# Earlier weight loads and a moved preparation of sink values in an attention + MoE + MLP kernel

## The chip, the cores and the metric

One Trainium2 chip, one core of it. The metric is the device time of one execution of the kernel, in microseconds (us), lower is better. Engines are called as the profile calls them: PE (TensorE, matrix products), DVE (VectorE), ACT (ScalarE), POOL (GpSimd), SP (SyncE, which here only issues DMAs).

## The reference

Three steps, all in float32; what one gives is the input of the next.

```python
# 1. attention: batch 2, 8 heads, 768 positions, head size 64
keep = (pos[None, :] < n_sink) | ((rel >= 0) & (rel < window))    # n_sink 4, window 128
a = softmax(where(keep, q @ k.T / 8, -1e9)); x = a @ v            # x: 1536 tokens x 512
# 2. mixture of 8 experts (512 -> 1024 -> 512), each token to its best one
active = x @ w_skip > 0; e = argmax(x @ w_gate); g = softmax(x @ w_gate)[e]
x[active] += g * (relu(x @ w1[e]) @ w2[e])
# 3. rational MLP, 512 -> 2048 -> 512
h = x @ w_in; out = (P3(h) / (1 + |b0||h| + |b1|h*h + 1e-6)) @ w_out
```

n_sink and window come as data. The kernel has a fast way for values that fit (n_sink up to 4, window up to 128) and a general one; a flag, `tripi`, chooses, and every engine loads it into a register (`values_load`) before the first scores.

## The kernel before, in words

The schedule is written by hand: instructions stand on each engine in the order in which the Python code emits them, and strings of steps such as `ORDER` set how steps of neighbouring units interleave.

**Attention** works on 8 pairs of heads. `attend(p)` runs from p = -2 to 10 and emits one round of `ORDER`, in which a step marked @-1 belongs to the pair before and @1 to the pair after. For a pair, PE transposes q and k (`tr`, tiles tq and tk), DVE and ACT copy them out of PSUM (`ev_q`, `ev_k`), POOL copies the four sink columns of K beside every later key tile (`k_sinks`), PE makes scores (`scores`, tile sc), DVE masks them and takes the row minimum (`mask_min`), ACT exponentiates (`expo`), PE transposes the result (`tr_p`, tile pt), and `pv` multiplies with v. The sinks' part of the product, `pv_sink`, needs the sinks' columns (copied by POOL into ps, transposed by `sink_t`) and the sinks' values v, spread over block rows: `sink_values` prepares these once for all pairs, as a PE product with a selection matrix (vsps <- sel), an ACT copy and a DVE subtraction into vsr, and four POOL multiplications by a mask of rows into vs. All of that stands ahead of the comparisons that make `tripi`. The rotated PSUM tiles with the tag tp (4 buffers) serve tq, tk, pt, vsps and the products alike.

At the start of `attend(p)`, SP issues the loads of q and k of pair p + 2 and whatever `after(u)` asks for (u = 2p and 2p + 1). The results go to DRAM (xd <- xs), per pair and half, and DVE or POOL adds up the router's logits lg.

**Routing** follows: DVE finds the best expert and the rank of each token, PE sums ranks (rkp, cntp), `slot_sel` compares ranks with a row of numbers for 12 token tiles (r; `SS` shares the tiles out: DVE up to SS[1] in groups of SS[0], POOL up to SS[2], ACT the rest), PE turns that into the token numbers of each expert's block (idps), and POOL gathers the first three blocks from xd (xblk).

**Experts**: 9 blocks of 128 tokens (8 experts and one for tokens beyond the first 128 of an expert). Each takes 8 chunks of weights of 512 KB (wch). Chunks 0, 1, ... go in order into rooms: s0 to s5 (`NSA` = 6, a pool that lives from the start), r0 to r9 (`NRING`), then s6 to s25 (`NSB` = 20, a pool `wsb` that lies where the attention's tiles were). After these 36, rooms r0 to r9, s24 and s25 are used again and again as their chunks have been used. 16 chunks are loaded in the attention (`after`, two per u from 7 to 14), 7 right behind it (`load_more(NPRE1 + NPRE2)`), 13 behind the gathers (`load_more(..., True)`: a memset by POOL, which stands behind the gathers in POOL's queue, holds the first of these loads, and the others follow it on SP).

Rooms s0 to s23 then take the MLP's weights (wc). These come as raw float64 words (raw, 512 KB each, 3 buffers), are turned by DVE into float32 (ta) and split by ACT and DVE into a high and a low part, one or a few per step from block 2 on. The MLP ends the kernel.

Of the kernel before, what the change touches and what calls it, by code (L numbers as in the profile page):

```python
# [9 lines left out]
F32 = mybir.dt.float32  # L10
F32R = mybir.dt.float32r
# [4 lines left out]
ALU = mybir.AluOpType  # L16
# [8 lines left out]
T = S // 128  # L25
# [11 lines left out]
EMPTY = 4096.0  # L37
ZROW = (E + NOV) * 128
NRING = 10
NSA = 6  # L40
NSB = 20
NCM = 24
ORDER = """
s0 Q1 e14@-1 c0@-1 s1 e15@-1 m00 O1@-2 K1 o0@-2 c1@-1 m10 p02@-1 O0@-2 p00@-1 P02@-1 p01@-1 m01 P00@-1 p12@-1 m11
# [1 line left out]
v4@-1 e12 v5@-1 e03 k0@1 w0@-1 s4 x0@-1 x1@-1 K0@1 s5 m04 e13 q0@1 x2@-1 g0@1 m05 e04 p10 Q0@1 q1@1 o1@-1 P10 m14 e05  # L46
m15 k1@1
"""
NPRE1 = 4
NPRE2 = 3  # L50
LAG = 3
PRE = 2
ML = 1
# [10 lines left out]
M0-3 M1-3 t0-4 A00 A10 P00 M2-3 A20 D00 D10 C30 C00 A5-1 t1-3 C40 t3-3 A30 C10 P1-1 A40 C20 D20 D30 D40  # L64
t2-3 C50 E00 g01
"""
SS = (4, 8, 10)
CRAW = 3
BLOCK = """
L2-1 G00 b03 L3-1 a00 o00 T00 U00 G10 V00 L40 x01 a10 T10 U10 F00 L50 F10 X01 V10 T20 U20 F20 F30 V20 L60 T30 U30  # L70
# [13 lines left out]
def emit(nc, tc, ctx, q, k, v, n_sink, window, w_skip, w_gate, w1, w2, w_in, w_out, pa, pb, out):  # L84
# [61 lines left out]
    def tokens_out(pr, half, ps, sb_pool, sb_tag, sb_bufs, eng=sp):  # L146

        b, c = divmod(pr, KC)
        n = T // 2
        xs = (sb_pool if eng is sp else xbp).tile(  # L150
            [128, n, 128], F32, tag=sb_tag if eng is sp else "xblk", name="xs", bufs=sb_bufs if eng is sp else 3
        )
        ls = sb_pool.tile([128, n, 2, E + 1], F32, tag=sb_tag + "l", name="ls", bufs=sb_bufs)
        r = ri[:, 2 * pr:2 * pr + 2, n * half:n * half + n].rearrange("p h (t o) -> p t h o", o=1)
        dve.tensor_tensor(
            xs.rearrange("p t (h d) -> p t h d", h=2), ps[:, :, 0:128].rearrange("p t (h d) -> p t h d", h=2),
            r.to_broadcast([128, n, 2, D]), op=ALU.mult,
        )
        dve.tensor_tensor(
            ls, ps[:, :, 128:NX].rearrange("p t (h e) -> p t h e", h=2), r.to_broadcast([128, n, 2, E + 1]), op=ALU.mult  # L160
        )
        l = lg4[:, b, half]
        eng_l = dve if pr == NPAIR - 1 and half else pool
        for h in range(2):
            eng_l.tensor_tensor(l, l, ls[:, :, h, :], op=ALU.add)
        r0 = (b * T + n * half) * 128
        eng.dma_start(xd[r0:r0 + n * 128, c * 128:(c + 1) * 128].rearrange("(t p) c -> p t c", p=128), xs)
# [24 lines left out]
    at.tile([128, T, KS], F32, tag="K", name="room", bufs=2)  # L192


    vs8 = at.tile([8, NPAIR, 128], F32, tag="P", name="vs8", bufs=4)
    vsr = at.tile([96, NPAIR, 128], F32R, tag="P", name="vsr", bufs=4)
    vs = at.tile([96, T - 2, NPAIR, 128], F32R, name="vs")

    rows = at.tile([96, T - 2], F32, name="rows")
    sel8 = at.tile([8, 3, 2, T - 2, 4], F32, name="sel8")  # L200
# [32 lines left out]
    def sink_values():  # L233
# [8 lines left out]
        for n in range(2):  # L242
# [5 lines left out]
            r = vsr[:, pr].rearrange("p a c -> p (a c)")  # L248
            act.copy(r, ps)
            dve.tensor_tensor(r[32:64], ps[32:64], r[32:64].bitcast(F32), op=ALU.subtract)  # L250
        for t in range(T - 2):
            pool.tensor_scalar(vs[:, t], vsr.bitcast(F32), rows[:, t:t + 1], None, op0=ALU.mult)

    Qt, Kt = {}, {}
    tp_cur = {}
# [124 lines left out]
    def pv_sink(pr):  # L380
        for t in range(T - 2):
            c, q0 = divmod(t, 2)
            q0 = 256 - 128 * c + 128 * q0
            pe.matmul(xps[pr][c][:, q0:q0 + 128], vs[:, t, pr, :], PS[pr], start=False, stop=t % 2 == 1)

    NU = 2 * NPAIR
    xT = {}
# [38 lines left out]
    def attend(p):  # L426
# [10 lines left out]
            load_v(p + 2)  # L437
        if p == 0:
            dve.tensor_scalar(upper, iota_r, pid, None, op0=ALU.is_gt)

# [31 lines left out]
    pool.memset(m1[:, 128:132], BIG)  # L474
    operands(1)
    k_sinks(0)
    sink_values()

    fast = ct([128, 1], F32, "fast")
    tripi = ct([128, 1], I32, "tripi")  # L480
# [65 lines left out]
    def after(u):  # L546
        if u == 0:
            router_loads()
        if u == 4:
            pab_loads()  # L550
        if NU - 9 <= u < NU:
            for _ in range(2):
                if len(wchunks) < NSA + NRING:
                    e, c = wq.pop(0)
                    load_chunk(e, c, w1[e], w2[e])

    for p in range(-2, NPAIR + 3):
        attend(p)
# [7 lines left out]
    def load_more(n, behind=False):  # L566

        for _ in range(n):
            e, c = wq.pop(0)
            load_chunk(e, c, w1[e], w2[e], behind=behind)  # L570
            behind = False
# [18 lines left out]
                tokens_out(pr, half, tokens_mm(pr, half, xTg[:, pr], gps, "g1"), gp, "gkeep", 1)  # L590
    gps_st.close()
    gp_st.close()
    load_more(NPRE1 + NPRE2)

    psr, psr_st = open_pool("psr", space=PSUM)
    psxt, psxt_st = open_pool("psxt", bufs=4, space=PSUM)
# [97 lines left out]

    for e in range(3):
        get_block(e, idx0[:, e:e + 1])
    load_more(NSB - NPRE1 - NPRE2, True)
    cnt9 = tk.tile([128, E1], F32, name="cnt9")
    dve.tensor_copy(cnt9, cntp)
    cnt, n_pass = cnt9[:, 0:E], cnt9[:, E:E1]  # L700
# [699 lines left out]
```

## Time and profile before

| what | value |
|---|---|
| median of 3 runs (lowest to highest) | 566.01 us (565.42 to 567.33) |
| the profiled execution | 566.55 us, of which its trace spans 564.8 us |
| mean granted clock of PE, as a share of full speed | 0.967 |
| busy share of the span: PE, DVE, ACT, POOL | 92%, 70%, 56%, 28% |
| DMA moved over the span | 83.52 MB, 148 GB/s on average |

Times inside the trace count from the span's start. A busy engine is one that has an instruction running; idle time ahead of an instruction is listed with what ended it. The attention lies at about 5 to 119 us, the routing at 119 to 134, the expert blocks at 134 to 280, the MLP from 268 to the end. PE is granted one of two clocks, 1.2 and 2.4 GHz, which a stretch's PEclk shows as 0.50 and 1.00.

### The profile page before, as it was taken

What the parts mean: (1) busy time and instruction counts of PE and PEld (TensorE: products, weight loads), DVE (VectorE), ACT (ScalarE), POOL (GpSimd) and SP (SyncE); (2) the same over time, 40 slices, a digit from 0 to 9 for tenths busy, and PEclk for the clock granted to TensorE, in tenths of its full rate; (3) what the DMA queues carried; (4) which work ended last, traced back from release to release, by engine and by line L of the source; (5) the groups of instructions that cost most, each with busy time, mean ns of one, the idle gap of its engine ahead of it and who ended that gap; (6) DMA issues with size and microseconds to landing.
All of it is one profiled execution on the core that took longest, in us unless ns stands there. A gap on an engine that the chain in (4) does not pass through costs nothing.

```text
span 564.8 us, 8147 instructions
## 1 busy us (share of the span) xinstructions
PE 517.7 (92%) x2800; PEld 404.2 (72%) x2800; DVE 392.8 (70%) x826; ACT 317.0 (56%) x648; POOL 160.2 (28%) x230
## 2 busy tenths in 40 slices
PE   4599999944999999988999979889999999999995
PEld 2488777734777777766687858678888888888883
DVE  3557767746013676655479999988987888987772
ACT  2568888810112333322557776757767677767671
POOL 2902111225610201011014334525333412522223
PEclk9989999975999999999999979989999999999998
DMA  8637899339999779999213112111000100100001
GB/s 168 133 72 147 238 270 319 126 115 397 314 272 362 269 274 385 415 411 389 102 58 111 57 37 93 39 37 57 19 20 19 38 1 2 74 1 0 1 0 74
DMA packets 73146, 83.52 MB, mean 148 GB/s; under 512 B 43977, under 2 KB 50121, under 8 KB 73098
## 3 DMA queue, kind: packets, MB, share of 16 engines
q1 hardware_dynamic: 67050, 69.41, 38.4%
q0 software_dynamic: 3664, 10.77, 5.8%
q10 hardware_dynamic: 2384, 2.76, 1.4%
q8 instruction: 24, 0.39, 0.3%
q14 instruction: 24, 0.20, 0.1%
HBM read 71.62 MB, written 11.29 MB: 147 GB/s over the span
## 4 chain that ended last, share of the span: by engine, by line
PE 32%; DVE 15%; issue 2%; ACT 2%; POOL 0%; POOLq 0%; DVEq 0%; ACTq 0%
PE hT L1106 16%; PE acc L1158 15%; DVE w L1146 2%; DVE w L1144 2%; DVE w L1131 1%; DVE p L1142 1%; DVE p L1140 1%; DVE p L1148 1%; DVE ta L847 1%; DVE ta L846 1%; DVE wc L833 1%; DVE ta L845 1%; DVE zx L956 1%; DVE zl L964 0%; POOL out L683 0%
## 5 line engine op out<-in xcount | busy, mean ns | idle before, releaser
L1106 PE MATMUL hT<-zh,wc 128*128 128x512 f32 x384 | 131.7, 404 | 5.2 <-DVE p L1142 3.3
L1134 POOL TENSOR_TENSOR gl<-p,gh 128x512 fp32r<-128x512 f32 x46 | 62.2, 1351 | 161.6 <-ACT gh L1126 72.0
L1158 PE MATMUL acc<-wc,gh 128*128 128x512 f32 x368 | 94.3, 397 | 1.2 <-ACT gh L1126 1.2
L1106 PEld LDWEIGHTS hT<-zh,wc 128*128 128x128 f32 x384 | 73.6, 192 | 22.5 <-DVE p L1142 3.5
L1158 PEld LDWEIGHTS acc<-wc,gh 128*128 128x128 f32 x368 | 69.8, 190 | 18.3 <-ACT gh L1126 1.6
L1106 PE MATMUL hT<-zl,wc 128*128 128x512 f32 x192 | 76.7, 399 | 3.2 <-DVE zl L964 3.2
L880 PEld LDWEIGHTS hps<-xbT,wch 128*128 128x128 f32 x576 | 68.4, 198 | 4.9 <-issue 3.6
L880 PE MATMUL hps<-xbT,wch 128*128 128x128 f32 x576 | 68.8, 282 | 0.7 <-ACT xbT L870 0.7
L891 PE MATMUL yps<-wch,hT 128*128 128x512 f32 x144 | 64.3, 594 | 2.2 <-ACT hT L885 2.2
L827 ACT CAST wc<-ta 128x512 fp32r<-128x512 f32 x32 | 19.7, 615 | 61.1 <-DVE ta L847 58.9
L1113 ACT ACTIVATE u<-hT 128x512 f32<-128x512 f32 x46 | 27.4, 596 | 43.5 <-PE hT L1106 43.2
L1158 PE MATMUL acc<-wc,gl 128*128 128x512 f32 x184 | 50.4, 393 | 0.0
L1131 DVE TENSOR_TENSOR w<-w,u 128x512 f32<-128x512 f32 x46 | 35.2, 765 | 20.9 <-ACT w L1117 17.5
L311 ACT ACTIVATE P<-P,rmin 128x260 f32<-128x260 f32 (+1 forms) x96 | 46.3, 487 | 4.4 <-DVE rmin L305 4.4
L891 PEld LDWEIGHTS yps<-wch,hT 128*128 128x128 f32 x144 | 26.4, 190 | 30.6 <-issue 27.3
L1106 PEld LDWEIGHTS hT<-zl,wc 128*128 128x128 f32 x192 | 36.8, 192 | 12.0 <-DVE zl L964 3.7
L1144 DVE SCALAR_TENSOR_TENSOR w<-w,cf,u 128x512 f32<-128x512 f32 x46 | 37.1, 806 | 8.8 <-ACT u L1123 8.5
L1158 PEld LDWEIGHTS acc<-wc,gl 128*128 128x128 f32 x184 | 34.5, 188 | 8.2 <-POOL gl L1134 0.2
L845 DVE TENSOR_SCALAR ta<-raw 128x512 int32<-128x512 int32 x32 | 13.8, 432 | 35.7 <-DMA raw<-in_moe_w_in 27.9
L1126 ACT CAST gh<-p 128x512 fp32r<-128x512 f32 x46 | 28.2, 613 | 18.3 <-DVE p L1148 18.3
L1117 ACT ACTIVATE w<-u,cf 128x512 f32<-128x512 f32 x46 | 37.5, 816 | 1.6
L1121 ACT ACTIVATE u<-w,cf 128x512 f32<-128x512 f32 x46 | 33.3, 723 | 9.2 <-DVE w L1131 9.2
(214 smaller groups left out, 855.8 us busy)
## 6 DMA issues: line engine op xcount, KB each, us to landing
wch<-in_moe_w SPq DMA_DIRECT2D x72, 512.0 KB
raw<-in_moe_w_in SPq DMA_DIRECT2D x16, 512.0 KB
raw<-in_moe_w_out SPq DMA_DIRECT2D x16, 512.0 KB
vraw<-in_v SPq DMA_DIRECT2D x8, 384.0 KB
qraw<-in_q SPq DMA_DIRECT2D x14, 192.0 KB
kraw<-in_k SPq DMA_DIRECT2D x14, 192.0 KB
xd<-xs SPq DMA_DIRECT2D x14, 192.0 KB
yd<-zero SPq DMA_DIRECT2D x1, 2560.0 KB
```

The lines of the kernel that those rows point to most:

```text
L311: act.activation(dst, dst, AF.Exp, scale=-1.0, bias=rmin[u][:, t:t + 1], accum_out=ssum[:, u, t:t + 1])
L880: pe.matmul(ps[:, j * 128:(j + 1) * 128], w[c][:, f:f + 128], xb[:, c, :], start=(c == 0), stop=(c == KC - 1))
L891: pe.matmul(y, hT[f // 4][:, (f % 4) * 128:(f % 4) * 128 + 128], w, start=(f == 0), stop=(f == KF1 - 1))
L1106: pe.matmul(ps, ww, zz[:, k_, :], start=(i == 0), stop=(i == 3 * KC - 1))
L1113: act.activation(tmps[n][0], h2[n], AF.Abs)
L1117: act.activation(w, u, AF.Identity, scale=b1_, bias=b0_)
L1121: act.activation(u, w, AF.Ln, bias=one6)
L1126: act.copy(gt[n][0], p)
L1131: dve.tensor_tensor(w, w, u, op=ALU.mult)
L1134: pool.tensor_tensor(gl, p, gh.bitcast(F32), op=ALU.subtract)
L1144: dve.scalar_tensor_tensor(w, w, one6, u, op0=ALU.add, op1=ALU.mult)
L1158: pe.matmul(acc[g, m], ww[:, m * 128:(m + 1) * 128], oo, start=(f == 0 and i == 0), stop=(f == KF2 - 1 and i == 2))
```

## The change

- `sink_values()` is no longer called ahead of the flag's comparisons but at the end of `attend(0)`; its four multiplications for all pairs (96 x 1024 each, one operand and a column of scalars) go, and `sink_rows(p)` makes the values of one pair at the end of `attend(p)`: one POOL tensor_tensor of 96 x 512 with both operands broadcast, into a tile vs with two buffers.
- 24 chunks are loaded in the attention: `CHUNKS` gives 0, 0, 3, 3, 3, 3, 6, 6 for the eight pairs. None is loaded between the attention and the gathers, 12 behind them. NSA is 14 and NSB 12, so rooms s0 to s13 take chunks 0 to 13, and r0 to r9 chunks 14 to 23.
- In `slot_sel`, DVE compares ten token tiles (two groups of five) instead of eight, POOL none instead of two, ACT two as before.
- The last pair's logits are added by DVE for both halves, not for one.

```diff
-NSA = 6
-NSB = 20
+NSA = 14
+NSB = 12
-NPRE1 = 4
-NPRE2 = 3
+CHUNKS = (0, 0, 3, 3, 3, 3, 6, 6)
-SS = (4, 8, 10)
+SS = (5, 10, 10)
-        eng_l = dve if pr == NPAIR - 1 and half else pool
+        eng_l = dve if pr == NPAIR - 1 else pool
-    vs8 = at.tile([8, NPAIR, 128], F32, tag="P", name="vs8", bufs=4)
-    vsr = at.tile([96, NPAIR, 128], F32R, tag="P", name="vsr", bufs=4)
-    vs = at.tile([96, T - 2, NPAIR, 128], F32R, name="vs")
+    vs8 = at.tile([8, NPAIR, 128], F32, name="vs8")
+    vsr = at.tile([96, NPAIR, 128], F32R, name="vsr")
...
-        for t in range(T - 2):
-            pool.tensor_scalar(vs[:, t], vsr.bitcast(F32), rows[:, t:t + 1], None, op0=ALU.mult)
+    vs = {}
+    def sink_rows(pr):
+        vs[pr] = at.tile([96, T - 2, 128], F32R, tag="vs", name="vs", bufs=2)
+        pool.tensor_tensor(
+            vs[pr], vsr[:, pr:pr + 1].bitcast(F32).to_broadcast([96, T - 2, 128]),
+            rows.rearrange("p (t o) -> p t o", o=1).to_broadcast([96, T - 2, 128]), op=ALU.mult,
+        )
...
         if p == 0:
             dve.tensor_scalar(upper, iota_r, pid, None, op0=ALU.is_gt)
+            sink_values()
+        if 0 <= p < NPAIR:
+            sink_rows(p)
...
     k_sinks(0)
-    sink_values()
...
-        if NU - 9 <= u < NU:
-            for _ in range(2):
-                if len(wchunks) < NSA + NRING:
-                    e, c = wq.pop(0)
-                    load_chunk(e, c, w1[e], w2[e])
+        if u % 2:
+            for _ in range(CHUNKS[u // 2]):
+                e, c = wq.pop(0)
+                load_chunk(e, c, w1[e], w2[e])
...
-    load_more(NPRE1 + NPRE2)
...
-    load_more(NSB - NPRE1 - NPRE2, True)
+    load_more(NSB, True)
```

How this moves instructions shows at three places. **The kernel's start.** On DVE, from the second part of q's copy for pair 0 (Q) on, before:

```order
L267 COPY Q<-tq 128x256
L234 TENSOR_REDUCE rows<-ident 96x4
L250 TENSOR_TENSOR vsr<-vsps,vsr 32x512 x2
L481 TENSOR_SCALAR fast<-nsf 128x1
L482 SCALAR_TENSOR_TENSOR fast<-nsf,fast 128x1
L483 SCALAR_TENSOR_TENSOR fast<-nsf,fast 128x1
L484 TENSOR_SCALAR tripi<-fast 128x1
L489 TENSOR_LOAD tripi
```

The same place of the changed kernel:

```order
L273 COPY Q<-tq 128x256
L489 TENSOR_SCALAR fast<-nsf 128x1
L490 SCALAR_TENSOR_TENSOR fast<-nsf,fast 128x1
L491 SCALAR_TENSOR_TENSOR fast<-nsf,fast 128x1
L492 TENSOR_SCALAR tripi<-fast 128x1
L497 TENSOR_LOAD tripi
```

The comparisons follow the copy at once; rows and the two subtractions into vsr now stand far behind, after the comparison `upper` and ahead of pair 1's second Q copy. On POOL, from the first copy of K's sink columns (pair 0) on, before (pid to one_c are constants, the second K copy is pair 1's, ps are pair 0's sink columns):

```order
L277 COPY K<-K 128x5x4
L239 COPY sel_114<-ident 8x16 x6
L252 TENSOR_SCALAR vs<-vsr,rows 96x1024 x4
L489 TENSOR_LOAD tripi
L493 IOTA pid 128x1
L495 IOTA iota_r 128x128
...
L512 MEMSET one_c 128x1
L277 COPY K<-K 128x5x4
L322 COPY ps_0_125<-P 128x16 x6
```

And of the changed kernel:

```order
L283 COPY K<-K 128x5x4
L497 TENSOR_LOAD tripi
L501 IOTA pid 128x1
L503 IOTA iota_r 128x128
...
L520 MEMSET one_c 128x1
L283 COPY K<-K 128x5x4
L237 COPY sel_113<-ident 8x16 x6
L255 TENSOR_TENSOR vs<-vsr,rows 96x512
L328 COPY ps_0_124<-P 128x16 x6
```

The constants and pair 1's K copy no longer stand behind the multiplications; ps of pair 0 stands behind that pair's own vs. PE's two products vsps move likewise, from ahead of the flag to behind pair 1's last transposes of k.

**SP in the attention's last two pairs**, from the v load of pair 7 on, before:

```order
L187 DMA vraw<-in_v 128x12x64
L537 DMA wch<-in_moe_w 128x1024 x2
L540 DMA wch<-in_moe_w 128x2x512 x2
L167 DMA xd<-xs 128x3x128 x2
L540 DMA wch<-in_moe_w 128x2x512 x2
L167 DMA xd<-xs 128x3x128 x4
```

And of the changed kernel:

```order
L186 DMA vraw<-in_v 128x12x64
L548 DMA wch<-in_moe_w 128x2x512 x4
L545 DMA wch<-in_moe_w 128x1024 x2
L166 DMA xd<-xs 128x3x128 x2
L545 DMA wch<-in_moe_w 128x1024 x2
L548 DMA wch<-in_moe_w 128x2x512 x4
L166 DMA xd<-xs 128x3x128 x4
```

Six chunks stand ahead of each of the two pairs of stores where four and two stood. All other loads of q, k and v stand ahead of these bursts.

**SP in the expert blocks**, from the raw loads 0 to 2 on (each row of wch from here on takes a room that has been used before; pb is the table of places), before:

```order
L821 DMA raw<-in_moe_w_in 128x512 x3
L540 DMA wch<-in_moe_w 128x2x512 x4
L537 DMA wch<-in_moe_w 128x1024 x4
L540 DMA wch<-in_moe_w 128x2x512 x2
L939 DMA pb<-pd 128x12x3
L821 DMA raw<-in_moe_w_in 128x512
L821 DMA raw<-in_moe_w_out 128x512 x4
L821 DMA raw<-in_moe_w_in 128x512 x3
L540 DMA wch<-in_moe_w 128x2x512 x2
```

And of the changed kernel:

```order
L827 DMA raw<-in_moe_w_in 128x512 x3
L548 DMA wch<-in_moe_w 128x2x512 x4
L545 DMA wch<-in_moe_w 128x1024 x2
L945 DMA pb<-pd 128x12x3
L827 DMA raw<-in_moe_w_in 128x512
L827 DMA raw<-in_moe_w_out 128x512
L545 DMA wch<-in_moe_w 128x1024 x2
L827 DMA raw<-in_moe_w_out 128x512
L548 DMA wch<-in_moe_w 128x2x512 x2
L827 DMA raw<-in_moe_w_out 128x512 x2
L827 DMA raw<-in_moe_w_in 128x512 x3
L548 DMA wch<-in_moe_w 128x2x512 x2
```

Raw loads 3 to 7 now stand among chunks 36 to 45, which wait for the rooms of chunks 14 to 23 instead of 6 to 15; up to chunk 47 the counts are equal again, and so is the order from there on.

## Rows read from the trace of the kernel before

**Rows 1.** Stretches: length, busy us of PE, PEld, DVE, ACT, POOL; PEclk; DMA share, GB/s.
```profile
14.00:16.00 2.00, 0.00 (x0) 0.00 (x0) 1.69 (x3) 0.73 (x2) 0.96 (x1) 1.00 0.10 15
...
60.00:80.00 20.00, 20.00 (x170) 16.31 (x170) 14.92 (x61) 15.84 (x52) 4.06 (x22) 1.00 0.88 233
...
130.00:140.00 10.00, 5.42 (x24) 5.05 (x25) 6.85 (x34) 0.59 (x1) 5.06 (x7) 0.50 1.04 415
...
180.00:200.00 20.00, 20.00 (x120) 14.89 (x119) 11.68 (x22) 4.54 (x8) 3.18 (x3) 1.00 0.79 268
...
200.00:220.00 20.00, 20.00 (x130) 15.66 (x129) 15.38 (x26) 8.04 (x14) 1.99 (x2) 1.00 0.87 320
...
220.00:240.00 20.00, 19.84 (x103) 13.27 (x102) 11.16 (x20) 6.13 (x11) 1.00 (x1) 1.00 1.04 411
```

**Rows 2.** Timeline of PE, 9 to 45: start, length, engine, line, operation, [idle before].
```profile
9.87 3.72 PE L245 MATMUL vsps<-vs,sel 8*96 8x512 f32 x4 [1.25 <-POOL sel L239]
...
17.13 3.85 PE L290 MATMUL sc<-K,Q 64*128 64x128 f32 x16 [3.53 <-DVE tripi L484]
...
27.87 0.71 PE L290 MATMUL sc<-K,Q 64*128 64x260 f32 x4 [2.88 <-DVE rmin L305]
...
28.51 0.33 PE L332 MATMUL pt<-ident,P 128*128 128x128 f32 x1
...
32.19 0.27 PE L350 MATMUL pt<-ident,ps 128*96 128x128 f32 x1
...
41.98 0.27 PE L332 MATMUL pt<-ident,P 128*128 128x128 f32 x1
...
43.95 0.27 PE L350 MATMUL pt<-ident,ps 128*96 128x128 f32 x1
```

**Rows 3.** Timeline of DVE, 8 to 17.
```profile
8.36 0.42 DVE L267 COPY Q<-tq 128x256 f32<-128x256 f32 x1
...
14.25 0.68 DVE L250 TENSOR_TENSOR vsr<-vsps,vsr 32x512 fp32r<-32x512 f32 x1 [1.02 <-ACT vsr L249]
...
15.15 1.01 DVE L482 SCALAR_TENSOR_TENSOR fast<-nsf,fast 128x1 f32<-128x1 f32 x1
...
16.39 0.15 DVE L484 TENSOR_SCALAR tripi<-fast 128x1 int32<-128x1 f32 x1
```

**Rows 4.** Timeline of POOL, 15 to 28.
```profile
15.04 11.32 POOL L252 TENSOR_SCALAR vs<-vsr,rows 96x1024 fp32r<-96x1024 f32 x4 [5.22 <-DVE vsr L250]
...
27.55 0.26 POOL L277 COPY K<-K 128x20 f32<-128x20 f32 x1
```

**Rows 5.** Timelines of DVE, POOL and PE, 119 to 134, sorted by time.
```profile
119.36 0.20 DVE L159 TENSOR_TENSOR ls<-xtps,ri 128x54 f32<-128x54 f32 x1
...
119.71 0.56 POOL L165 TENSOR_TENSOR lg<-lg,ls 128x27 f32<-128x27 f32 x2 [7.71 <-DVEq L580]
...
123.73 1.29 DVE L646 TENSOR_TENSOR r<-iota_r,rk 128x512 bf16<-128x512 f32 x2
...
123.89 2.12 POOL L652 TENSOR_SCALAR r<-iota_r,rk 128x128 bf16<-128x128 f32 x2 [0.32 <-DVE rk L640]
...
127.22 1.30 POOL L676 DMA_INDIRECT xblk<-xd,idx  x1 [1.22 <-DVE pre L707]
...
133.91 1.09 PE L865 MATMUL xtr<-ident,xblk 128*128 128x128 f32 x4 [7.59 <-DMA xblk<-xd,idx]
```

**Rows 6.** Timeline of SP, whose rows are the issues of DMAs.
```profile
122.13 1.79 SPq L537 DMA_DIRECT2D wch<-in_moe_w  x4
```

**Rows 7.** A later gather alone: timeline of POOL, and a stretch (columns of rows 1).
```profile
410.52 1.43 POOL L676 DMA_INDIRECT zy<-yd,yix  x1
...
414.00:414.25 0.25, 0.25 (x3) 0.20 (x2) 0.25 (x1) 0.25 (x1) 0.00 (x0) 1.00 0.00 0
```

**Rows 8.** Waits of PE: engine, line, waited for: us in total, times, longest.
```profile
PE yps L891 <- ACT hT L885: 2.2, 2, 2.0
...
PE hT L1106 <- ACTq L1254: 2.0, 1, 2.0
```

More of the change, by code (lines that the diff above doesn't have):

```diff
@@ L383, in pv_sink @@
             q0 = 256 - 128 * c + 128 * q0
-            pe.matmul(xps[pr][c][:, q0:q0 + 128], vs[:, t, pr, :], PS[pr], start=False, stop=t % 2 == 1)
+            pe.matmul(xps[pr][c][:, q0:q0 + 128], vs[pr][:, t], PS[pr], start=False, stop=t % 2 == 1)
     NU = 2 * NPAIR
```

## Prediction

> **What bounds the kernel now.** I read the stretches first, then PE's timeline wherever PE was idle, then the engine that released it. In the steady attention PE is busy 20.00 of 20 us while DVE, ACT and POOL have room [rows 1]; in the expert blocks it is busy 20.00 or 19.84 of 20 up to 240 us. So a change gains only where PE stands, and there are three such places ahead of 140 us.
>
> The first is the start. PE begins the scores at 17.13, after 3.53 us idle, when the flag `tripi` is there [rows 2]. DVE had copied Q by 8.78, but the flag's comparisons stand behind the second subtraction into vsr, which waits for ACT, which waits for PE's vsps of 9.87 to 13.59 [rows 2, 3].
>
> The second is at 27.87, where the scores of pair 1 come after 2.88 us idle. The row names DVE as releaser; but these scores read K's sink columns, whose POOL copy ran from 27.55 to 27.81, right ahead of them, because four multiplications held POOL from 15.04 to 26.36 [rows 2, 4]. Behind this idle time PE is slow: the transposes pt from 28.51 to the one of ps at 32.19 take 3.68 us, the same piece of the next pair (41.98 to 43.95) 1.97.
>
> The third is the routing. PE stands 7.59 us for the first gather, issued at 127.22, before its transpose starts at 133.91 [rows 5]. SP began to issue the seven loads behind the attention at 122.13 [rows 6], and in 130 to 140 the DMA engines are full (share 1.04, 415 GB/s) [rows 1].
>
> **The change part by part.** The sum is made against the profiled execution, 566.55 us, which lies 0.54 above the median of the runs.
>
> *Flag.* The four comparisons follow the Q copy at 8.78. They took from 14.96 to 16.54, of which 1.01 is one that began just after POOL's multiplication (15.04); its neighbour takes 0.15 [rows 3, 4]. With the usual step of 0.2 the flag is there at about 9.6; PE started 0.59 after it, so now at 10.2: **7.0 us** gained. If the slow comparison stays, 6.2. What is late next would be data: PE wants q and k of pair 1 right behind the first scores, whose row lasts 3.85 us [rows 2], so at about 14.0. All first loads, those of v behind them included, are over by about 14.3, since the DMA share falls to 0.10 in 14 to 16 [rows 1]; q and k stand ahead of two v loads of 384 KB each, so I take no wait, at most 0.3.
>
> *Second stall.* POOL's multiplications are gone from ahead of the K copy, so 2.88 us of idle time go, and 3.68 - 1.97 = 1.7 of slow transposes if PE no longer stands there long: 4.6. Against it, vsps is now in PE's busy stretch: 3.72 us for four records in the slow start [rows 2]; at the full clock I take half, 1.9. Behind it, pair 1's second Q copy waits on DVE for the two subtractions (0.68 each), and the first pt needs the PSUM buffer that this copy empties: about 0.7. Net **2.0 us**. Bounds: 4.6 - 1.9 = 2.7, and 2.88 - 3.72 - 0.7 = -1.5 if vsps stays slow and so do the transposes.
>
> *Values pair by pair.* A multiplication of 96 x 512 has half the elements of one of the four, 11.32 / 4 / 2 = 1.4 us [rows 4]. POOL is busy 4.06 of 20 us in the steady attention [rows 1], so 1.4 per pair fits; pair 0's must end before its ps copies, and these before PE's transpose of ps, where I find 0.2 us to spare; twice the price would cost 1.2. What it can also cost is the hold-up that the slow comparison showed, 0.86 us of DVE. Between none and 8 x 0.86 = 6.9 I take **0.3 lost**, since DVE has 5 of 20 us free and of the four old multiplications one shows such a row.
>
> The Trainium skill, page "SBUF — State Buffer", section "Who interferes with whom", says that a VectorE instruction with two SBUF inputs and a GpSimd one that reads SBUF exclude each other for a whole instruction. By it a hold-up could last the full 1.4 us of a multiplication, eight times 11.2, which would make it 564.4; the slow row agrees in kind. Most DVE work of the attention reads PSUM and one SBUF operand, which by the same section does not collide.
>
> *Last pair's logits.* DVE's ls ends at 119.56 and POOL's two additions at 120.27 [rows 5]; DVE's own two take about 0.4: **0.3**, between 0 and 0.5.
>
> *Rank comparison.* POOL's two tiles ended at 126.01; DVE's two groups (1.29 us) end at 125.02 and with 640 instead of 512 columns at about 125.34 [rows 5]. Seven instead of three small products follow: **0.4**, between 0 and 0.7.
>
> *Loads.* The seven loads of 512 KB leave the gather's way; by the same place the changed kernel's 24 chunks must have landed. The last two pairs last 23.5 us by the pitch of the ps transposes (43.95 - 32.19 = 11.76 [rows 2]); their twelve chunks bring 6.3 MB, 268 GB/s; the steady attention with its short q and k pieces averaged 233 at share 0.88, and 320 to 411 GB/s are moved elsewhere [rows 1], so they are down before the routing. A gather alone: issue at 410.52, no traffic any more from 414.0, at most 3.5 us [rows 7]. With 0.1 to PE's start the 6.69 us from issue to transpose become 3.6: **3.1**, between 0 and 3.3. The twelve loads behind the gathers still wait for POOL to issue all three, so they come too late to hurt the first.
>
> *Expert blocks.* PE is full there and chunks 0 to 23 suffice for three blocks, so nothing is gained or lost at their start. Later raw loads arrive late: in 220 to 240 the DMA share is 1.04, and PE waits 2.2 and 2.0 us behind ACT, which stands in conversions [rows 1, 8]. From chunk 46 on SP's order is the same, so I take 0; the bounds are these waits gone, +4.2, or doubled, -4.2. The MLP is untouched.
>
> Sum: 7.0 + 2.0 - 0.3 + 0.3 + 0.4 + 3.1 = 12.5. 566.55 - 12.5 = 554.05, and 0.54 below it for the median: **553.5 us**.
>
> **The rivals.** *The gather is as slow as before*, because its 6.7 us are its own or the twelve loads behind it catch it: 553.5 + 3.1 = 556.6. For it: three gathers are issued together, the quiet one alone. Against it: rows 7.
>
> In the Trainium skill, page "DMA: Bandwidth & Descriptors", section "Queues, rings and completion order", each DMA engine takes turns between queues packet by packet. By that the gather did not stand behind all seven loads and loses less by them, which speaks for this rival; no row here shows packets of one queue between those of another.
>
> *DVE is held up in every pair* by POOL's two-input work: 553.5 + 6.9 - 0.3 = 560.1. For it the one slow row, against it that the other rows of that stretch are not slow.
>
> *The start doesn't give what it says*: vsps slow, transposes slow, and an early load late: 553.5 + 3.5 + 0.3 = 557.3.
>
> *Expert blocks shift* by their late conversions, either way: 549.3 or 557.7.
>
> *The other sign: the rooms come free too late.* Chunks 36 to 45 wait for the chunks of blocks 1 and 2, one block later than before, and five raw loads stand among them. If DMA then lies idle and these fifteen loads fall into the full stretch from 220 on, each costs 0.524 MB / 411 GB/s = 1.28 us: 19 us, 572.7. It decides from twelve of the fifteen on (12.5 + 1.7). Against it: before, the share is 0.79 in 180 to 200 and 0.87 in 200 to 220 [rows 1], 6.8 us free, eight chunks fewer are left to load when the gathers are issued than were left when SP began the seven, and chunk 36 is wanted only in block 4.
>
> **How the numbers follow.** The forecast with its terms as worked out has 0.62; slow gather 0.12; expert blocks 0.13; start 0.05; DVE 0.05; rooms 0.03. The range takes in the expert blocks both ways, the slow gather and the start, and stops short of a combination of these: 549.3 to 558.5. About 0.3% (1.7 us) is what a measurement of this kernel can tell from no change. Only the last rival, or the start together with DVE and a slow gather, ends above 564.3: faster 0.95, same 0.02, slower 0.03.
>
> **What would show it.** In the changed profile the first scores start near 10.2; PE has no idle time of over 1 us ahead of pair 1's scores, and the first transpose of ps comes near 23 (32.19 - 9.0); POOL has eight rows vs of about 1.4 us. The last products of the attention end 8.7 earlier; from the first gather's issue to the first transpose xtr there are about 3.6 us; the expert blocks start about 12.5 earlier, and so do the MLP and the end. The prediction is wrong if the scores wait for q or k of pair 1, if DVE's rows beside vs lengthen in every pair, or if PE waits in blocks 2 to 4 for conversions.

## The result and the profile of the changed kernel

The changed kernel takes 552.47 us (median of 4 runs, 551.56 to 553.36), the kernel before beside it 565.71 (4 runs, 565.19 to 567.33): a ratio of 0.9761, 95% interval 0.9735 to 0.9787. The forecast was 553.5, range 549.3 to 558.5. The profiled execution took 551.56 (span 549.8); a repeat in a later group, with its own runs of the kernel before, gave 0.9751 (0.9708 to 0.9794).

The same marks in both traces show where the 15.0 us between the two profiled spans come from. "Forecast" is the running sum of the prediction's terms.

| mark | before | after | earlier by | forecast |
|---|---|---|---|---|
| first scores of pair 0 | 17.13 | 10.18 | 6.95 | 7.0 |
| first transpose of ps, pair 0 | 32.19 | 22.65 | 9.54 | 9.0 |
| last products of the attention (xps) | 115.12 | 105.58 | 9.54 | 8.7 |
| row mx, the routing's first | 120.54 | 111.24 | 9.30 | 9.0 |
| first gather issued | 127.22 | 117.10 | 10.12 | 9.4 |
| first transpose xtr | 133.91 | 120.83 | 13.08 | 12.5 |
| MLP's first products hT | 268.20 | 255.52 | 12.68 | 12.5 |
| stop of PE for zl in the MLP | 368.68 | 353.68 | 15.00 | 12.5 |
| end of the span | 564.8 | 549.8 | 15.0 | 12.5 |

Executions differ, at the start above all. A second profile of each kernel (experiments 10 and 12) puts the same marks 6.63 apart at the first transpose of ps, 9.86 at xtr, 10.51 at the MLP's first products, 12.57 at the stop for zl and 13.6 at the end.

The start, in the timeline of PE of the changed kernel; it answers to [rows 2]:

```profile
10.18 3.74 PE L296 MATMUL sc<-K,Q 64*128 64x128 f32 x16 [1.53 <-ACT iw L493]
13.85 1.11 PE L266 MATMUL tk<-ident,kraw 128*128 128x128 f32 x4
...
17.62 1.93 PE L243 MATMUL vsps<-vs,sel 8*96 8x512 f32 x4
19.48 0.93 PE L296 MATMUL sc<-K,Q 64*128 64x128 f32 x8
20.34 0.33 PE L338 MATMUL pt<-ident,P 128*128 128x128 f32 x1
...
22.65 0.27 PE L356 MATMUL pt<-ident,ps 128*96 128x128 f32 x1
```

From 10.18 on no row has a bracket of idle time: the keys of pair 1 are there when PE wants them (13.85), and vsps takes 1.93 inside the busy stretch. The timelines of DVE and POOL there, sorted by time, answer to [rows 3, 4]:

```profile
9.10 0.16 DVE L491 SCALAR_TENSOR_TENSOR fast<-nsf,fast 128x1 f32<-128x1 f32 x1
9.29 0.15 DVE L492 TENSOR_SCALAR tripi<-fast 128x1 int32<-128x1 f32 x1
15.92 0.20 POOL L283 COPY K<-K 128x20 f32<-128x20 f32 x1 [4.50 <-ACT K L279]
20.11 1.04 POOL L255 TENSOR_TENSOR vs<-vsr,rows 96x512 fp32r<-96x512 f32 x1 [3.19 <-DVE vsr L248]
20.20 0.68 DVE L248 TENSOR_TENSOR vsr<-vsps,vsr 32x512 fp32r<-32x512 f32 x1 [0.18 <-ACT vsr L247]
```

K's sink columns are copied at 15.92, well before the scores want them. A row vs takes 1.04, and DVE's subtraction right beside it 0.68, as without it. The routing, from the timelines of DVE, POOL and PE, answers to [rows 5]:

```profile
111.24 0.25 DVE L620 TENSOR_REDUCE mx<-lg 128x12 f32<-128x96 f32 x1 [0.69 <-DVEq L587]
...
114.22 1.56 DVE L652 TENSOR_TENSOR r<-iota_r,rk 128x640 bf16<-128x640 f32 x2
...
117.10 1.28 POOL L682 DMA_INDIRECT xblk<-xd,idx  x1 [2.83 <-DVE pre L713]
...
120.83 1.09 PE L871 MATMUL xtr<-ident,xblk 128*128 128x128 f32 x4 [4.64 <-DMA xblk<-xd,idx]
122.59 6.36 PE L886 MATMUL hps<-xbT,wch 128*128 128x128 f32 x32 [0.67 <-ACT xbT L876]
...
129.10 3.82 PE L886 MATMUL hps<-xbT,wch 128*128 128x128 f32 x32
```

From issue to transpose there are 3.73 us instead of 6.69. What is new to read: the first 32 products hps take 6.36, the next 32 take 3.82. The stretches of PE (columns: us; PE busy; granted clock; DMA share; GB/s) show why:

```profile
112.00:114.00 2.00, 0.86 (x24) 1.00 0.00 0
...
118.00:120.00 2.00, 0.00 (x0) 0.50 0.37 121
...
126.00:128.00 2.00, 2.00 (x11) 0.52 1.03 301
128.00:130.00 2.00, 2.00 (x29) 1.00 0.90 278
```

After PE has stood (no row of it from 118 to 120), the granted clock is at its lower level (0.50, 1.2 GHz) and comes back only during the first products.

### The profile page after: what moved, and what is told of

Its sections match the earlier page's. It is cut to its first block, busy times and chain, and to the rows that moved or that the text cites. A ratio compares the mean times of both kernels' runs of the same rounds, so it can differ in the third digit from the quotient of the medians.

```text
span 549.8 us, 8138 instructions
## 1 busy us (share of the span) xinstructions
PE 513.1 (93%) x2800; PEld 400.8 (73%) x2800; DVE 392.4 (71%) x828; ACT 316.6 (58%) x648; POOL 154.4 (28%) x230
## 4 chain that ended last, share of the span: by engine, by line
PE 33%; DVE 15%; ACT 2%; issue 2%; POOL 0%; POOLq 0%; DVEq 0%; ACTq 0%
PE hT L1112 17%; PE acc L1164 16%; DVE w L1152 2%; DVE w L1150 2%; DVE p L1148 2%; DVE w L1137 2%; DVE p L1146 1%; DVE p L1154 1%; DVE ta L853 1%; DVE ta L852 1%; DVE wc L839 1%; DVE ta L851 1%; DVE zx L962 1%; DVE zl L970 0%; POOL out L689 0%
## 5 line engine op out<-in xcount | busy, mean ns | idle before, releaser
L1164 PE MATMUL acc<-wc,gh 128*128 128x512 f32 x368 | 93.2, 394 | 0.0
L1112 PEld LDWEIGHTS hT<-zl,wc 128*128 128x128 f32 x192 | 36.9, 192 | 12.5 <-DVE zl L970 3.9
L839 DVE TENSOR_TENSOR wc<-ta,wc 128x512 fp32r<-128x512 f32 x32 | 22.2, 693 | 22.7 <-ACT wc L833 21.3
```

Source lines behind the costliest of these rows:

```text
L839: dve.tensor_tensor(lo, v_, hi.bitcast(F32), op=ALU.subtract)
L1112: pe.matmul(ps, ww, zz[:, k_, :], start=(i == 0), stop=(i == 3 * KC - 1))
L1164: pe.matmul(acc[g, m], ww[:, m * 128:(m + 1) * 128], oo, start=(f == 0 and i == 0), stop=(f == KF2 - 1 and i == 2))
```

## The experiments

Each group of four kernels ran beside its own runs of the kernel before (medians 567.4 to 567.9 us), so ratios are compared. Most of their intervals reach 0.4 to 0.5% to either side, 2 to 3 us, so a smaller difference rests on the rows of one execution of each kernel. Theory A is the prediction's: the gain is the sum of three stops of PE taken away. The rivals were that one edit carries it all, that the loads' place is of no account, and, after the first trace, that 2.3 us of it came by chance.

**1. The sinks' values early again.**

```diff
         if p == 0:
             dve.tensor_scalar(upper, iota_r, pid, None, op0=ALU.is_gt)
-            sink_values()
...
     k_sinks(0)
+    sink_values()
```

> The changed kernel with one thing put back: the sinks' values (vsps, vsr) are worked out ahead of the flag again; their spreading stays pair by pair. My theory: DVE reaches the flag some 7 us later, so the first scores start near 17.1 instead of 10.18, but vsps (1.9) and the late first pt (0.7) go back into PE's idle time; K's sink columns are still copied in time, so there is no idle time ahead of pair 1's scores. 552.5 + 7.0 - 1.9 - 0.7 = 556.9 us, and the transposes pt of pair 0 quick. Rival one: the idle time of 2.88 ahead of pair 1's scores was DVE's, as its row said, and comes back: 559.8. Rival two: the order of the flag carries the whole gain of the start: 552.5 + 9.5 = 562.0.

Measured: 556.15, ratio 0.9791 (0.9753 to 0.9829). Its timelines of PE and DVE, sorted by time:

```profile
15.05 0.16 DVE L490 SCALAR_TENSOR_TENSOR fast<-nsf,fast 128x1 f32<-128x1 f32 x1
...
16.17 3.85 PE L296 MATMUL sc<-K,Q 64*128 64x128 f32 x16 [2.66 <-DVE tripi L492]
20.93 1.15 PE L296 MATMUL sc<-K,Q 64*128 64x260 f32 x8
...
26.80 0.27 PE L356 MATMUL pt<-ident,ps 128*96 128x128 f32 x1
```

The transpose of ps comes 26.80 - 22.65 = 4.15 later than in the changed kernel (expected 4.4), and pair 1's scores have no idle time. So the stop at 27.87 of the kernel before came from POOL's multiplications. DVE, which its row named, had itself waited for POOL: `upper`, ahead of pair 1's Q copy, needs iota_r, one of the constants behind the multiplications. DVE of the kernel before:

```profile
26.69 1.07 DVE L439 TENSOR_SCALAR upper<-iota_r,pid 128x128 bf16<-128x128 f32 x1 [1.58 <-POOL iota_r L495]
```

Two ways lead from POOL to the stop, the K copy (to 27.81) and this row with the row minimum behind it (to 27.77); no run parts them. Of the 9.54 us at the start 5.4 are the freed POOL and 4.15 the order of the flag; the profile of the kernel before and this one both have a vsps of 3.72, and beside a vsps of 1.95 the order of the flag would be worth less. The scores start at 16.17 rather than 17.13 mostly because the slow comparison is gone: 0.16, where POOL has no long multiplication behind vsr. The MLP starts 3.97 later than in the changed kernel; the ratios of this run and of the repeat below differ by 0.0040, 2.3 us, with intervals that overlap, so the size rests on the marks.

**2. Four pairs' values at once.**

```diff
-        vs[pr] = at.tile([96, T - 2, 128], F32R, tag="vs", name="vs", bufs=2)
+        vs[pr] = at.tile([96, T - 2, 128], F32R, tag="vs", name="vs", bufs=4)
...
             sink_values()
+            for pr in range(4):
+                sink_rows(pr)
-        if 0 <= p < NPAIR:
+        if 4 <= p < NPAIR:
             sink_rows(p)
```

> The changed kernel with the values of pairs 0 to 3 spread at once behind pair 0's sinks, the others pair by pair as before. POOL is then held for 4 x 1.04 = 4.2 us instead of 1.04 there. My theory: POOL's copies into ps of pair 0 stand behind it, so PE's transpose of ps of pair 0 comes 3.1 us late and nothing gives it back: 552.5 + 3.1 = 555.6 us, with an idle time of PE of that size ahead of the first transpose of ps. Rival one: PE has enough other work there, under 0.5: 552.5 to 553.0. Rival two: the idle time also slows PE for some us, as in the kernel before: 552.5 + 3.1 + 1.7 = 557.3.

Measured: 555.11, ratio 0.9782 (0.974 to 0.9823). Timelines of POOL and PE:

```profile
19.37 4.03 POOL L255 TENSOR_TENSOR vs<-vsr,rows 96x512 fp32r<-96x512 f32 x4 [2.57 <-DVE vsr L248]
23.34 0.86 POOL L328 COPY ps<-P 128x16 f32<-128x16 f32 x6
24.26 0.31 PE L356 MATMUL pt<-ident,ps 128*96 128x128 f32 x1 [0.63 <-POOL ps L328]
```

The place is right: the copies into ps stand behind the four rows, and PE waits for them. The size is smaller: vsps lay 0.77 earlier in this execution, so the transpose came 1.61 + 0.77 = 2.4 later, not 3.1. The changed kernel has slack there: POOL's row ends at 21.15, its copies some 0.86 later, and PE asks at 22.65. The idle time is only 0.63: the transposes ahead of it ran at a lower granted clock here (0.57 in 20 to 22, 0.58 in 22 to 24, against 1.00).

**3. The loads as before** (16 chunks in the attention, seven ahead of the gathers).

```diff
-NSA = 14
-NSB = 12
+NSA = 6
+NSB = 20
...
-        if u % 2:
-            for _ in range(CHUNKS[u // 2]):
+        if NU - 9 <= u < NU:
+            for _ in range(2):
...
     gp_st.close()
+    load_more(7)
...
-    load_more(NSB, True)
+    load_more(NSB - 7, True)
```

> The changed kernel with the loads of weights as in the kernel before: 16 chunks in the attention, seven ahead of the gathers, thirteen behind; start and routing as changed. My theory: the first gather shares the DMA engines with the seven loads again, and from its issue to PE's transpose xtr there are 6.7 us instead of 3.73: 552.5 + 3.0 = 555.5 us, the expert blocks as much later and otherwise alike. Rival one: the gather's time depends on other things, within 0.5 of 552.5. Rival two: the earlier loads also moved the waits of the expert blocks, and those change by up to 4.2 either way: 551.3 to 559.7.

Measured: 556.42, ratio 0.981 (0.9769 to 0.9851). Timelines of POOL and PE:

```profile
117.03 1.28 POOL L684 DMA_INDIRECT xblk<-xd,idx  x1 [2.82 <-DVE pre L715]
...
123.60 1.08 PE L873 MATMUL xtr<-ident,xblk 128*128 128x128 f32 x4 [7.48 <-DMA xblk<-xd,idx]
```

6.57 from issue to transpose against 3.73: 2.84 us, where 3.0 was expected. The first products hps start 2.77 later, the MLP 3.75; what the blocks lose on the way, 1.0, is left open.

**4. The routing edits undone.**

```diff
-SS = (5, 10, 10)
+SS = (4, 8, 10)
...
-        eng_l = dve if pr == NPAIR - 1 else pool
+        eng_l = dve if pr == NPAIR - 1 and half else pool
```

> The changed kernel with the two routing edits put back: the last pair's second addition of logits on POOL again, and the ranks compared as 4, 4 and two tiles on POOL again. One theory, the prediction's: the additions cost PE's way 0.3 when on POOL, the comparison 0.4, so the gathers come 0.7 later: 553.2 us. The rival, from the changed kernel's trace, in which the row mx came only 9.30 us earlier where the attention's products came 9.54 earlier: the logits give nothing or lose 0.24 and the comparison gives 0.6, so that putting both back costs 0.3 to 0.4: 552.8. Times can't tell these apart; the rows between the last products and mx, and between rk and the first gather, can.

Measured: 554.45, ratio 0.9774 (0.9734 to 0.9815). Timelines of DVE and POOL:

```profile
111.35 0.25 DVE L620 TENSOR_REDUCE mx<-lg 128x12 f32<-128x96 f32 x1 [0.97 <-POOLq L587]
...
114.70 2.11 POOL L658 TENSOR_SCALAR r<-iota_r,rk 128x128 bf16<-128x128 f32 x2 [0.31 <-DVE rk L646]
...
118.03 1.30 POOL L682 DMA_INDIRECT xblk<-xd,idx  x1 [1.22 <-DVE pre L713]
```

From the last xps (105.94) to mx there are 5.41 us; in the changed kernel 111.24 - 105.58 = 5.66. So the moved additions cost 0.25. In both kernels mx starts only behind the branch at line 587: 0.27 after POOL's last addition, which ends at 111.08, but 0.70 after DVE's own, which ends at 110.54. Counted from the last xps DVE's additions end 0.18 earlier than POOL's, and 0.43 are lost behind them. From rk to the gather 3.79 us against 3.18: the rank comparison gives 0.6. The rival, from the trace, was right.

**5. Four loads ahead of the gathers.**

```diff
     gp_st.close()
+    load_more(4)
...
-    load_more(NSB, True)
+    load_more(NSB - 4, True)
```

> The changed kernel with four of the twelve loads behind the gathers issued ahead of them, right after the attention, where the DMA engines stand empty from 112 to 118. Theory one: four loads of 512 KB at 400 GB/s take 5.2 us and are down before the gather at 117, which stays at 3.73 from issue to transpose; all later loads come some 5 us of DMA time earlier, and the waits of PE behind ACT's late conversions (2.4 and 2.0 in the changed kernel) go in part: 550.5, between 549 and 552.5. Rival one: the later loads are bound by rooms that come free, not by DMA time, and nothing changes: 552.5. Rival two: they still hit the gather: 553.5 to 555.5.

Measured: 553.69, ratio 0.9762 (0.9725 to 0.9799), the same as the changed kernel's. The gather, issued at 116.75, takes 5.25 to the transpose; the DMA share is 0.81 from 116 to 117, where the changed kernel has 0.00, so four loads meet it too. The MLP starts 0.65 later than in the changed kernel though the blocks start 1.17 later. Rival two, and half of it is given back.

**6, 7, 8. PE kept busy in the routing.**

```diff
+    hot = psr.tile([128, 512], F32, tag="hot", name="hot")
+
+    def keep_hot(n):
+        for _ in range(n):
+            pe.matmul(hot, upper, ones.rearrange("p (o c) -> p o c", o=1).to_broadcast([128, 4, 128]), start=True, stop=True)
+
+    keep_hot(16)
...
+    keep_hot(3)
...
+    keep_hot(18)
```

The 16 stand ahead of rkp (8 in the other two runs), the 3 behind cntp, the 18 behind idps.

> The changed kernel with 37 bf16 products of 128 x 512 added that nobody reads, in the places in which PE stands in the routing: 16 behind the last logits, 3 behind the counts, 18 behind the products of the slots. In the changed kernel the granted clock is 0.50 from 116 to 126, the first four transposes xtr take 1.09 us and the first 32 products hps 6.36, where the same rows at the full clock take 0.60 and 3.8. My theory: this loss of 0.5 + 2.6 = 3.1 us comes from PE's standing before, and with PE busy the clock stays at 1.0: 552.5 - 3.1 = 549.4 us. Rival one: the clock falls all the same, and nothing changes: 552.5. Rival two: the added products stand in front of the real ones on PE and hold them up by up to 1 us each time: 550 to 554 with the clock at 1.0.

Measured: 555.2, ratio 0.9822 (0.9768 to 0.9877). The clock stayed at 1.00 from 110 to 130 and hps took 3.84. But PE began the added products at 110.95, behind the branch, and they held the ranks' products from 113.02 to 114.40. So 8 were tried with the four loads, and then alone:

> The four loads ahead of the gathers together with added products in the routing, of which the first group is cut from 16 to 8 so that they end before the ranks' products are ready. With 16 the clock stayed at 1.0 and the 32 products hps fell from 6.36 to 3.84 us, but the ranks' products started 1.38 later, and PE waited 4.3 instead of 2.4 us in the expert blocks for ACT. Theory one: the blocks start as in the changed kernel, at 122.6 or 0.5 earlier, and the 2.5 us of hps are gained; since the loads are no longer late, the blocks keep it: 549, between 547.5 and 550.5. Rival one: the expert blocks are bound by the DMA engines from 200 to 250, and all that is gained ahead of them is given back in waits for conversions: 551.5 to 552.5.

> The changed kernel with the added products in the routing (8, 3 and 18) alone, without the four loads ahead of the gathers. Theory one, that the expert blocks are bound by the DMA engines and their late conversions: the 32 products hps take 3.84 instead of 6.36 us and the clock is 1.0, but the MLP's first products come at 255.0 to 256.0 as in the changed kernel, and PE waits 2 us more in the blocks; no difference that can be measured. Rival: the blocks keep what is gained ahead of them, the MLP begins near 253.0 and the time is 2.5 us shorter.

Measured: with the four loads 552.52, ratio 0.9732 (0.9685 to 0.978); alone 554.74, ratio 0.9779 (0.9733 to 0.9829): neither differs from the changed kernel by more than the intervals. PE of the run alone:

```profile
120.68 0.63 PE L880 MATMUL xtr<-ident,xblk 128*128 128x128 f32 x4 [0.69 <-DMA xblk<-xd,idx]
121.99 3.84 PE L895 MATMUL hps<-xbT,wch 128*128 128x128 f32 x32 [0.67 <-ACT xbT L885]
...
255.96 0.50 PE L1121 MATMUL hT<-zh,wc 128*128 128x512 f32 x1 [2.38 <-ACTq L1269]
```

The 2.5 us are gained at 126 and gone at 255.96 (changed kernel: 255.52), in the run alone already at 148. Behind hps three products idps wait there for DVE's rows `room` (0.39, 0.34 and 0.34), and the first products yps start 1.57 earlier than in the changed kernel (131.62 against 133.19). Then the 64 products hps of the second block take 9.25 us (138.49 to 147.74) where the changed kernel's take 7.14 (140.06 to 147.20), with four stops of PE for nothing that the trace names; the longest:

```profile
144.47 0.49 PE L895 MATMUL hps<-xbT,wch 128*128 128x128 f32 x2 [0.35 <-issue]
```

Behind them PE is 0.54 later than in the changed kernel. What these stops are is left open; theory one's time came out here without its mechanism. The run with four loads has no such stops: there the first products yps start 1.87 earlier (131.32 against 133.19), and still do at 219.91 against 221.78. Then, changed kernel (DVE, ACT, PE):

```profile
234.19 0.43 DVE L851 TENSOR_SCALAR ta<-raw 128x512 int32<-128x512 int32 x1 [3.62 <-DMA raw<-in_moe_w_in]
...
236.10 0.62 ACT L833 CAST wc<-ta 128x512 fp32r<-128x512 f32 x1 [6.26 <-DVE ta L853]
...
238.11 0.60 ACT L891 ACTIVATE hT<-hps 128x512 f32<-128x512 f32 x1 [0.42 <-ACT ys L904]
238.76 1.55 PE L897 MATMUL yps<-wch,hT 128*128 128x512 f32 x3 [1.82 <-ACT hT L891]
```

and with the four loads and the added products (DVE, PE):

```profile
234.11 0.43 DVE L861 TENSOR_SCALAR ta<-raw 128x512 int32<-128x512 int32 x1 [3.90 <-DMA raw<-in_moe_w_in]
...
238.67 1.61 PE L907 MATMUL yps<-wch,hT 128*128 128x512 f32 x3 [3.61 <-ACT hT L901]
```

The raw load lands at the same time in both, PE comes 1.87 earlier and waits 1.79 longer. Chain: load, DVE's extraction, ACT's cast, and behind that cast in ACT's order the hT which PE needs. In the run alone the same row of PE comes at 238.86. So a gain ahead of the expert blocks that lasts until there ends there.

**9. The ten rooms of the ring early again.**

```diff
-    rooms = [f"s{n}" for n in range(NSA)] + [f"r{n}" for n in range(NRING)] + [f"s{n}" for n in range(NSA, NSA + NSB)]
+    rooms = [f"s{n}" for n in range(6)] + [f"r{n}" for n in range(NRING)] + [f"s{n}" for n in range(6, NSA + NSB)]
```

> The changed kernel with one line different: the ten rooms that are loaded a second time hold the chunks 6 to 15 again, as in the kernel before, instead of 14 to 23, so they come free one block earlier. The prediction's rival of the other sign said that rooms which come free late cost time; the changed kernel's DMA engines do stand idle from 158 to 162. Theory one: this idle time is what the blocks lack later, and with the rooms free earlier the waits for ACT's conversions (2.4 and 2.0) go in part: 551, between 550 and 552.5. Rival: conversions need rooms of their own, of which some then come free later, and nothing is gained or up to 1 is lost: 552.5 to 553.5.

Measured: 553.96, ratio 0.9748 (0.9707 to 0.9788): no difference. The DMA share from 160 to 165 is 1.06 where the changed kernel has 0.56 (1.04 from 163 to 168, since the blocks of this profile, that of the slowest execution, start 3.2 later). So the rooms did make that idle time; no cost of it shows. What fixes the arrival at 234 beyond a DMA share of 1.03 from 200 on is left open.

**10, 11, 12. The 2.3 us of the MLP.** Between the first products acc and the stop for zl the kernel before takes 82.33 us, the changed one 80.01, though nothing there was edited. DVE of the kernel before:

```profile
288.12 0.69 DVE L833 TENSOR_TENSOR wc<-ta,wc 128x512 fp32r<-128x512 f32 x1 [0.69 <-ACT wc L827]
291.96 0.69 DVE L1131 TENSOR_TENSOR w<-w,u 128x512 f32<-128x512 f32 x1 [3.14 <-issue]
```

"issue" is a wait for nothing that the trace shows.

> The kernel before, unchanged, profiled once more. In its first profile DVE stood 3.14 us for nothing that the trace names ahead of its row at 291.96, and the stretch from the first products acc to the second stop for zl lasted 82.33 us, where the changed kernel and all four variants of it so far show 79.9 to 80.4. Theory one: the stop is a chance of that execution, so it is not there again, the stretch lasts about 80, and 2.3 us of the 15.0 by which the changed profile is shorter are no gain of the change. Theory two: it belongs to the kernel before, is there again at the same row, and the change took it away.

Measured: 566.92 (one run); the stretch 82.34, the row again, with 3.14, at 291.05. It belongs to the kernel. In both profiles it ends 1.75 us after a packet of instruction queue 14 (290.2 and 289.3). In experiment 4 such a stop of 2.04 lies one row further on, ahead of p at 279.90, 1.8 after a packet at 278.1, and its stretch is 82.00. That kernel has 826 instructions on DVE, as the kernel before; the changed one has 828, and its stop, now 1.34, lies two rows ahead of that p, at wc, where DVE would have waited 0.69 for ACT anyway. The two more are the additions of the last pair's logits, which POOL made before. (The profile's count leaves out branches and semaphores, so it is no exact address: with the same 826 the stop lies ahead of w in one kernel and ahead of p in the other.) The row of the changed kernel:

```profile
276.07 0.69 DVE L839 TENSOR_TENSOR wc<-ta,wc 128x512 fp32r<-128x512 f32 x1 [1.34 <-ACT u L1119]
```

So only the place of the code was shifted:

```diff
             dve.tensor_scalar(upper, iota_r, pid, None, op0=ALU.is_gt)
+        if p == 3:
+            for _ in range(12):
+                dve.memset(shift, 0.0)
...
+    shift = ct([128, 1], F32, "shift")
```

> The kernel before with 12 memsets of 128 x 1 added on DVE in the attention of pair 3, which nobody reads and which take under 1 us there, so that all of DVE's later code lies 12 instructions further on. Both profiles of the kernel before have a stop of DVE of 3.14 us ahead of the same instruction, which ends 1.75 us after a packet of an instruction queue, and the stretch from the first products acc to the second stop for zl lasts 82.33 us. Theory one: DVE waits there for its code, whose blocks end at a fixed number of instructions. Shifted by 12, the end of the block falls into the rows early, where DVE waits for ACT anyway: no stop of over 1 us from 280 to 300, the stretch 80.0, and 2.3 us less than the kernel before: 0.996 of its time. Theory two: the stop belongs to the instruction or to the DMA traffic there, not to the code's place: 82.3 again and the same time.

Measured: 565.20 against 567.71, ratio 0.9955 (0.9928 to 0.9981); 0.996 was expected. The stretch is 80.08, and DVE's row w in the same place reads:

```profile
292.85 0.69 DVE L1135 TENSOR_TENSOR w<-w,u 128x512 f32<-128x512 f32 x1 [0.72 <-ACT w L1121]
```

Twelve instructions that nobody reads make the kernel before 2.5 us faster by its times. (The one profile of it starts the MLP 3.4 later than the first profile of the kernel before, so its span of 564.2 is no measure; the stretch and the ten runs are.) That the wait is for code is what fits the shift and the packets; the trace has no row that says so. The Trainium skill, page "Runtime: NRT & Kernel Launch", section "Instruction fetch mechanics", says that an engine's code comes in blocks through its own DMA queue while it executes, and that crossing a block's end is mostly hidden. Code that comes in blocks agrees with the shift; "mostly hidden" does not hold for this stop, at 3.14 us, if it is such a crossing.

The changed kernel once more:

> The changed kernel once more, unchanged, beside the others of this group. Its first profile shows 5.73 us from the first products of the slots to the transpose xtr, the MLP's first products at 255.52 and 80.0 us from acc to the second stop for zl. Theory one: all this is fixed by the program and comes again within 0.3. Theory two: the stretch of the expert blocks is bound by DMA and varies by up to 1 us between executions.

Measured: 553.59, ratio 0.9751. From the gather to xtr 3.75, the stretch 80.29, both as in its first profile (3.73 and 80.01). But the first transpose of ps came at 23.55 and the MLP at 256.76: the start differs by 0.9 between executions, and what follows with it. The stretches show a granted clock of 0.50 from 22 to 24 there and 1.00 in the first profile.

## Why the prediction was right, point by point

- **Flag, 7.0:** 6.95, in part by luck. The four comparisons follow the Q copy at the step of 0.2, none is slow, and the scores start 0.89 after tripi began. In the two other profiles with the order of before they start at 15.36 and 15.47 instead of 17.13, since vsps took 1.95 there instead of 3.72; against those executions the term would be 5.2 or 5.3. The base of the sum was an execution with a slow vsps.
- **Second stall, 2.0:** 9.54 - 6.95 = 2.6, near the upper bound of 2.7. Between the second profiles of both kernels this and the flag come to 6.63 together, not 9.54. The prediction saw POOL's K copy behind the stop and not DVE's own wait for POOL at `upper`. vsps costs 1.93 as said (1.9); the 0.7 for the late Q copy are at most 0.34, since from pt to ps there are 2.31 us against 1.97 in a later pair [rows 2].
- **Values pair by pair, -0.3:** 0. A row takes 1.04, not 1.4: the price was scaled by elements from the old form, and the new form, which spreads both operands in one instruction, is cheaper than that. No hold-up: the marks keep the same 9.54 from 22.65 to 105.58. The slow comparison was POOL's doing all the same. It comes again in the second profile of the kernel before (DVE and POOL):

```profile
13.27 8.49 POOL L252 TENSOR_SCALAR vs<-vsr,rows 96x1024 fp32r<-96x1024 f32 x3 [3.45 <-DVE vsr L250]
13.38 1.01 DVE L482 SCALAR_TENSOR_TENSOR fast<-nsf,fast 128x1 f32<-128x1 f32 x1
14.43 0.16 DVE L483 SCALAR_TENSOR_TENSOR fast<-nsf,fast 128x1 f32<-128x1 f32 x1
```

  and goes in experiment 1 (0.16). The page "SBUF — State Buffer" of the Trainium skill, section "Who interferes with whom", says that a DVE instruction with two SBUF inputs contends with a GpSimd one that reads SBUF, and that one with at most one such input, outside some modes of DVE, does not. The trace agrees with both: the comparison reads two tiles in SBUF and was held 0.85 us, the subtraction with one input in PSUM, beside vs at 20.11, was not. It does not show the wait for a whole instruction that the prediction took from this page: a multiplication lasts 2.83, and the next comparison, of the same form, took 0.16 beside it.
- **Last pair's logits, +0.3:** wrong in sign, -0.25 (experiment 4). The step that failed took the end of the last addition as what mx waits for; mx waits for the branch at line 587 behind it, which costs 0.70 behind DVE's own addition and 0.27 behind POOL's.
- **Rank comparison, +0.4:** 0.6 by experiment 4, within its bounds. From the last xps to xtr the two routing edits give 0.64 together (105.94 to 121.83 against 105.58 to 120.83); 0.21 of it lie between mx and rk (2.89 against 2.68), where the second profile of the changed kernel has 2.89 too.
- **Loads, +3.1:** 2.96 between the profiles, 2.84 by experiment 3. The rival by which the gather does not stand behind the loads fell. Experiment 5 shows the middle: four loads cost 1.5.
- **Expert blocks, 0:** -0.4. PE's waits behind ACT come to 2.4 and 2.0 instead of 2.2 and 2.0 [rows 8], so they neither went nor doubled. The rival of the rooms did not come; the DMA engines stood idle near 160 at no cost that shows.
- **"The MLP is untouched":** the step that failed. Its code was, its place was not: +2.3, which the forecast has no term for. With both routing edits undone the stretch is 82.00 again, and the only instructions that DVE then has fewer are the last pair's two additions: by these counts the edit that loses 0.25 in the routing is also the one that moves the stop in the MLP to where it costs little. Without the 2.3 the first profiled spans would differ by 12.7, next to the 12.5 of the sum, but the medians of the two groups differ by 13.24 and 14.12, which leaves 10.9 and 11.8 for what the sum put at 12.5. So two errors of opposite sign, a start taken from an execution with a slow vsps and an MLP put at nothing, have their share in 553.5 lying so near 552.47.

## What to carry to other kernels

Look at what stands ahead of a short instruction on its own engine: a flag of four tiny comparisons behind a wait cost 5 to 7 us, a copy of 0.2 us and a row of constants behind four multiplications another stop, and the engine that the row names as releaser may itself have been waiting. A transfer that waits for nobody belongs behind one for which PE waits, and even four loads of 512 KB ahead of a gather are felt. Before buying time ahead of a stage, ask what ends last in that stage: here 1.87 us that PE was ahead, with the clock kept up, were waited for again at one late raw load. And when times are compared, an edit of two instructions on an engine can move a stop far behind them.

## What the runs showed of the hardware that was not expected

- A stop of DVE of 3.14 us (two profiles of the kernel before) at one place of its code, which moves and shrinks when the number of instructions ahead of it changes: 82.0 to 82.3 us for the stretch with 826 instructions (three profiles), 79.9 to 80.4 with 828 (the changed kernel and its other variants), 80.08 with 838. That it is a wait for code is inferred.
- PE at a granted clock of 0.50 for some us near the start in some executions of one kernel and not in others: mean clock from 10 to 34 of 0.93, 0.79 and 0.72 in the three profiles with the order of before, 1.00 in eight of the eleven of the changed kernel and its variants, 0.79 to 0.93 in the other three.
- vsps at the start took 3.72 in two executions (the kernel before, experiment 1) and 1.95 in two others (the kernel before again, and shifted) with the same granted clock of 1.00 shown from 9 to 11, so the clock's row doesn't tell all of PE's speed there.
